# A top-k attention with a gated feed-forward: the feed-forward's steps in a fixed list over four slots

## The chip, the core and the metric

The kernel runs on one core of a Trainium2 chip, in one launch. Five engines run side by side, each through its own queue of instructions in the order in which the program issues them: TensorE (PE; PEld are its weight loads), VectorE (DVE), ScalarE (ACT), GpSimd (POOL) and SyncE (SP), which here issues DMAs. Where one engine needs what another makes, it waits on a semaphore. The metric is the device time of one execution in microseconds; lower is better. Three runs of the kernel before took 1398.21, 1399.92 and 1400.42 us, median 1399.92.

## What is computed

```python
batch, n_heads, seq, head_dim = (8, 8, 576, 64)
scores = scale * np.matmul(q, k.transpose(0, 1, 3, 2))
kth = np.partition(scores, -top_k, axis=-1)[..., -top_k:-top_k + 1]
scores = np.where(scores >= kth, scores, -1000000000.0)
attn = np.exp(scores - max); attn = attn / (sum + 1e-09)
x = (attn @ v), heads side by side        # 4608 tokens x 512
h = x @ w_in                              # 512 x 2048
g = h * np.cos(h)
out = g @ w_out                           # 2048 x 512
```

top_k is 32 of 576 keys. All is in fp32 (the weights are decoded on the chip from 64-bit words in the first slots).

## The kernel before

**Units, slots and blocks.** A unit is 128 tokens and one pair of heads (hp, 0 to 3): 144 units. Four units make a block of 128 tokens: 36 blocks. `slot(i, u, w, x, z)` (line 755) is called for i = 0 to 143, and its order of calls is the order in each engine's queue. Below, m = i mod 4. A slot carries several units at different stages: u = unit i is searched, w = unit i-1 is masked and exponentiated, x = unit i-2 is sent, z are the units whose values are due (from the second block on, a block's four units, in the slot with m = 2 three slots after that of its last unit).

**Attention, by engine.** `scores` (line 235, PE) writes two heads' scores of a unit into the PSUM tile `sc` (two buffers) and their last columns into `rim`, one PSUM tile of two banks whose rest holds the values of a block; from unit 4 on two units are scored together, in the slots with m = 0 and 2. `take_scores` (line 250, ACT) copies them into `s`: line 253 from `sc`, line 257, two instructions, from `rim`. VectorE folds the 576 scores of a row in two, `rest` (line 267, larger ones) and `low` (smaller ones, by two GpSimd passes, lines 283 and 292), and searches four rounds of eight in `rest` and two in `low` with MAX8 and MATCH_REPLACE8 (lines 359 and 364). One slot's search is most of VectorE's work, and the merge of line 347 opens the next. In slots 8 to 10 (`BUSY`) VectorE makes `low` itself. `mask` (line 374, ACT) sets apart what lies under the 32nd score and scales the small `nd`; `exponentials` (line 383, ACT) follow. `send` (line 740): GpSimd copies the result into `halves` (line 410) and the reciprocal of the sums beside it (line 412), SP writes that to DRAM (line 441), and a transposing DMA (line 447) brings it back into `ring`. From there PE forms the `values` (line 456) in `rim`, and `take_values` (VectorE, lines 491 and 499) multiplies them by the reciprocals into `xT`, in the `ahead` call between the two searches of `low`.

**The feed-forward.** Per block: four banks of the first product (`ff1`, line 554; two halves of a bank by two calls; PSUM tile `mm`), each taken by two ACT passes (`take_first`, lines 568 and 570: h in turns into `g`, the same rounded into `x` as an integer); for each pair of banks, 1024 columns, GpSimd converts the integer (line 590), subtracts it from g (line 599), ACT takes the sine (line 609; it needs another activation table than the exponentials, so a table load stands before it and before the next exponentials), GpSimd multiplies (`gate`, line 616). The second product (`ff2`, line 630; PSUM tile `o2`) sums sixteen pieces; two calls, 16 matmuls, are called a group here. `take_second` (lines 640 and 642, ACT) copies the result and issues its store on ACT's own DMA queue. `mm` and `o2` share two PSUM buffers, so that while `o2` is open one buffer is left for the banks.

**What sets the order.** Calls to `feed` at fixed places in the slot (`plan`, line 748) ask for steps of the first (0) or second (1) product; `can_first` and `can_second` (lines 647 and 655) grant them when the block is ready, weights are decoded and gates lie some ticks back; the second product is granted from slot 10 on (`ff["now"] < 2 * NP + 3`, with `now` = i + 1). Full banks wait in a queue for `take_banks`, which is called at several places; `reduce_first`, `reduce_second`, `sines` and `gate` take what is next. In the slots with odd i `sines(1)` stands ahead of `mask`. All of this is decided in Python while the program is built. After the last slot `drain` and `forward` (lines 825 and 815) work off the rest; there VectorE takes the place of GpSimd.

Of the kernel before, what the change touches and what calls it, by code (L numbers as in the profile page):

```python
# [30 lines left out]
def kernel(  # L31
# [64 lines left out]
    ff = {"live": 0, "tick": 0, "now": 0, "end": False, "kind": 0, "half": 0, "open": 0, "late": False}  # L96
# [213 lines left out]
    def topk_first(u, w):  # L310

        u["top"] = tops[u["n"] % len(tops)]
        if w:
            merge_first(w)
        if u["n"] not in BUSY:
            fold_sum(u)
        fold_high(u)
        if w:
            merge_second(w)
        if u["n"] in BUSY:  # L320
            fold_now(u)
        topk_round(u, 0, [lambda: distances(w), lambda: None] if w else ())
# [82 lines left out]
    def split(u):  # L405
# [3 lines left out]
        halves = work.tile([P, 2, 2 * S + P], U16, tag="halves", name="halves", bufs=1)  # L409
        nc.gpsimd.tensor_copy(out=halves[:, :, 0 : 2 * S], in_=s.rearrange("p (k h) -> p h k", h=2))  # L410
        rden = u.pop("rden").bitcast(U16).rearrange("p (j h) -> p h j", h=2)
# [4 lines left out]
        u["halves"] = halves  # L416
# [64 lines left out]
    def take_values(us):  # L481
# [23 lines left out]
        blk["left"] -= n  # L505
        blk["tick"] = ff["tick"]


    widths = [P] * (B * S // P)
    blocks, block_of = [], {}  # L510
    t0 = 0
    for w in widths:
        blk = {"t0": t0, "w": w, "left": 0, "g": [], "gated": []}
        for u in units:
            if t0 <= u["tok"] < t0 + w:
                block_of[u["tok"]] = blk
                blk["left"] += 1
        blocks.append(blk)
        t0 += w


    first = deque((blk, i) for blk in blocks for i in range(2 * NF * blk["w"] // 512))
    second = deque(
        (blk, i, f) for blk in blocks for i in range(blk["w"] // P) for f in range(0, NF, 2)
    )
    fresh = deque()
    waiting = deque()
    sined = deque()
    full = deque()

    def open_bank():

        if ff["open"] + len(full) == 2:
            take_banks()
        ff["open"] += 1

    def ff1(blk, i):
        w = blk["w"]
        nf = 256 // w
        part = i % 4  # L540
        if part == 0:
            blk["g"].append(ffw.tile([P, 1024], F32, tag="g", name="g", bufs=CHUNKS))
            blk["x"] = ffw.tile([P, 1024], F32, tag="x", name="x", bufs=XB)
            ff["live"] += 1
        if part % 2 == 0:
            open_bank()
            blk["mm"] = ps.tile([P, 512], F32, tag="mm", name="mm", bufs=2)
        g, mm = blk["g"][-1], blk["mm"]
        for a in range(nf):
            f = i * nf + a  # L550
            at = (part % 2 * nf + a) * w
            for c in range(NC):
                for r0 in range(0, P, D):
                    nc.tensor.matmul(  # L554
                        mm[r0 : r0 + D, at : at + w],
# [5 lines left out]
        if part % 2 == 0:  # L561
            return
        ff["open"] -= 1
        full.append((take_first, blk, g, blk["x"], mm, part // 2))

    def take_first(blk, g, x, mm, half):
        at = slice(half * 512, half * 512 + 512)
        nc.scalar.mul(out=g[:, at], in_=mm, mul=INV_2PI / UP)  # L568

        nc.scalar.activation(  # L570
            out=x[:, at].bitcast(I32), in_=mm, func=AF.Identity, bias=quarter, scale=INV_2PI / UP
        )
        if half == 1:
            fresh.append([blk, g, x, False, ff["now"] if ff["late"] else 0])

    def take_banks():
        while full:
            take, *what = full.popleft()
            take(*what)

    def reduce_first():

        if not fresh or (ff["late"] and not ff["end"] and fresh[0][4] == ff["now"]):
            return
        g, x = fresh[0][1:3]
        fresh[0][3] = True
# [5 lines left out]
        )  # L592

    def reduce_second():
        if not fresh or not fresh[0][3]:
            return
        blk, g, x, *_ = fresh.popleft()
        if not ff["end"]:
            nc.gpsimd.tensor_tensor(out=x, in0=g, in1=x, op=ALU.subtract)  # L599
        waiting.append((blk, g, x, ff["now"]))  # L600

    def sines(least):

        n = sum(c[3] < ff["now"] for c in waiting)
        if n == 0 or (n < least and waiting[0][3] + 2 > ff["now"]):
            return
        for _ in range(n):
            blk, g, x, _ = waiting.popleft()
            nc.scalar.activation(out=x, in_=x, func=AF.Sin, bias=halfpi, scale=TWO_PI_BELOW)
            sined.append((blk, g, x))  # L610

    def gate(n):
        for _ in range(min(n, len(sined))):
            blk, g, x = sined.popleft()
            eng = nc.vector if ff["end"] else nc.gpsimd
            eng.tensor_tensor(out=g, in0=g, in1=x, op=ALU.mult)  # L616
            blk["gated"].append(ff["tick"])

    def ff2(blk, i, f0):
        w = blk["w"]  # L620
        if f0 == 0:
            open_bank()
            blk["o"] = ps.tile([P, 512], F32, tag="mm", name="o2", bufs=2)
        o = blk["o"]
        per = 1024 // w
        for f in range(f0, f0 + 2):
            g = blk["g"][f // per]
# [275 lines left out]
```

## Time and profile before

| | |
|---|---|
| runs | 1398.21, 1399.92, 1400.42 us |
| profiled execution | 1399.15 us, span of its instructions 1397.0 us |
| granted TensorE clock | 0.974 of full on the mean, 1.00 from 120 us on |
| ACT, POOL busy | 1140.6 us (82%), 1169.3 us (84%) |
| DMA | 240.86 MB, mean 172 GB/s |

A row of the timeline gives the start in us from the span's first instruction, the duration, the engine, the line, the operation, the tiles written and read, their shapes, and how many instructions it merges; in brackets the idle time of the engine just before and what ended it. A row of a group gives busy time in us, the mean of one in ns, and idle time before them in total. A row of a stretch gives busy time and (in brackets) the number of instructions of PE, PEld, DVE, ACT and POOL, then the granted clock, the DMA engines' share and GB/s.

### The profile page before, as it was taken

Reading aid. Unit: us, or ns where it says so; the run is one execution under the profiler, and the core shown is the slowest. Engines: PE = TensorE matmul, PEld = TensorE weight load, DVE = VectorE, ACT = ScalarE, POOL = GpSimd, SP = SyncE. Lnnn points to the kernel's source line nnn. Section 1 sums busy time; section 2 is a strip of 40 time slices with the busy share of each in tenths; the row PEclk is TensorE's granted clock in tenths of the full one; section 3 lists DMA queues with packets and bytes.
Section 4 is the critical chain, followed back from the end, with each engine's and each line's share of the span. In section 5 each row is a group of like instructions: output and inputs, shape, how many; then the busy total and the mean of one; then the engine's idle time right before and its main releaser. Section 6 shows DMA issues by size and latency. Waiting matters only on the chain.

```text
span 1397.0 us, 43804 instructions
## 1 busy us (share of the span) xinstructions
PE 1339.6 (96%) x17024; PEld 905.7 (65%) x17024; DVE 1334.2 (96%) x5004; ACT 1140.6 (82%) x2043; POOL 1169.3 (84%) x804
## 2 busy tenths in 40 slices
PE   5558999999999999999999999999999999999998
PEld 3445666666666666666666666666666666666664
DVE  7999999999999999999999999999999999999931
ACT  7987888888888888888888888888888888888842
POOL 4778988889988888888988889888888898998820
PEclk6688999999999999999999999999999999999999
DMA  9566776777575586658756567676766566555530
GB/s 303 180 203 179 196 191 167 202 175 206 160 179 160 154 198 177 175 161 200 185 157 170 159 178 191 177 164 171 211 163 172 160 171 163 160 146 157 157 103 16
DMA packets 427487, 240.86 MB, mean 172 GB/s; under 512 B 375952, under 2 KB 392592, under 8 KB 427280
## 3 DMA queue, kind: packets, MB, share of 16 engines
q1 hardware_dynamic: 420720, 224.22, 61.0%
q10 hardware_dynamic: 6560, 13.85, 2.9%
q8 instruction: 133, 2.18, 0.7%
q14 instruction: 74, 0.61, 0.1%
HBM read 45.09 MB, written 101.19 MB: 105 GB/s over the span
## 4 chain that ended last, share of the span: by engine, by line
PE 59%; DVE 35%; ACT 2%; DMA 2%; POOL 1%; issue 1%; SPq 0%; DVEq 0%; POOLq 0%; ACTq 0%
PE o L630 23%; PE mm L554 23%; DVE top L359 16%; DVE rest L364 10%; PE rim L475 7%; PE sc L242 5%; DVE low L364 3%; DVE rest L267 3%; PE rim L242 1%; DMA ring<-rows 1%; DMA rows<-halves 1%; DVE xT L491 0%; DVE top L347 0%; DVE w_out L151 0%; DVE top L352 0%
## 5 line engine op out<-in xcount | busy, mean ns | idle before, releaser
L554 PEld LDWEIGHTS mm<-xT,w_in 128*64 128x64 f32 x9216 | 512.8, 137 | 85.1 <-issue 57.2
L554 PE MATMUL mm<-xT,w_in 128*64 128x128 f32 x9216 | 528.7, 273 | 3.2 <-DVE xT L491 2.1
L630 PE MATMUL o<-w_out,g 128*64 128x512 f32 x2304 | 520.0, 594 | 0.0
L359 DVE MAX8 top<-rest 128x8 f32<-128x288 f32 x1152 | 479.5, 452 | 0.0
L364 DVE MATCH_REPLACE8 rest<-top,rest 128x288 f32<-128x288 f32 x864 | 377.0, 444 | 0.0
L378 ACT ACTIVATE s<-s,top 128x576 f32<-128x576 f32 x288 | 207.7, 768 | 160.8 <-DVE top L352 157.8
L630 PEld LDWEIGHTS o<-w_out,g 128*64 128x64 f32 x2304 | 158.6, 137 | 254.1 <-issue 253.1
L410 POOL COPY halves<-s 128x2304 uint16<-128x2304 uint16 x140 | 294.8, 2106 | 29.1 <-ACT s L387 26.0
L359 DVE MAX8 top<-low 128x8 f32<-128x288 f32 x576 | 242.6, 452 | 0.4 <-POOL low L292 0.4
L387 ACT ACTIVATE s<-s,nd 128x576 f32<-128x576 f32 x288 | 220.5, 769 | 1.1
L292 POOL TENSOR_TENSOR low<-low,rest 128x576 int32<-128x576 int32 x141 | 199.6, 1416 | 11.1
L283 POOL TENSOR_TENSOR low<-s 128x576 int32<-128x576 int32 x141 | 199.7, 1417 | 6.1 <-ACT s L259 6.1
L599 POOL TENSOR_TENSOR x<-g,x 128x1024 f32<-128x1024 f32 x68 | 161.6, 2376 | 5.7
L242 PE MATMUL sc<-k,q 64*64 64x448 f32 (+1 forms) x1120 | 146.9, 568 | 16.9 <-DVE low L275 10.2
L616 POOL TENSOR_TENSOR g<-g,x 128x1024 f32<-128x1024 f32 x68 | 161.7, 2378 | 0.0
L475 PE MATMUL rim<-ring,v 128*64 128x128 f32 (+1 forms) x2560 | 138.3, 267 | 0.0
L475 PEld LDWEIGHTS rim<-ring,v 128*64 128x64 f32 x2560 | 129.2, 139 | 6.5 <-issue 6.0
L253 ACT COPY s<-sc 128x896 f32<-128x896 f32 (+1 forms) x144 | 128.4, 891 | 3.1 <-PE sc L242 3.1
L257 ACT COPY s<-rim 64x256 f32<-64x256 f32 (+1 forms) x280 | 102.9, 368 | 29.5 <-PE rim L475 27.9
L364 DVE MATCH_REPLACE8 low<-top,low 128x288 f32<-128x288 f32 x288 | 125.8, 446 | 0.0
L267 DVE TENSOR_TENSOR rest<-sc,s 128x576 f32<-128x576 f32 x144 | 107.7, 748 | 7.0 <-ACT s L259 6.4
L568 ACT ACTIVATE g<-mm 128x512 f32<-128x512 f32 x144 | 85.2, 592 | 25.7 <-PE mm L554 23.2
(55 smaller groups left out, 1161.8 us busy)
## 6 DMA issues: line engine op xcount, KB each, us to landing
rows<-halves SPq DMA_DIRECT2D x140, 640.0 KB, 3.5
out_dram<-ob ACTq DMA_DIRECT2D x36, 256.0 KB, 2.2
q<-in_q_dram SPq DMA_DIRECT2D x31, 288.0 KB, 4.6
st<-in_moe_w_in_dram SPq DMA_DIRECT2D x16, 512.0 KB, 5.1
v<-in_v_dram SPq DMA_DIRECT2D x32, 256.0 KB, 4.2
k<-in_k_dram SPq DMA_DIRECT2D x31, 144.0 KB, 4.2
k<-in_k_dram SPq DMA_DIRECT2D x32, 128.0 KB, 4.7
st<-in_moe_w_out_dram SPq DMA_DIRECT2D x8, 512.0 KB, 4.7
```

The lines of the kernel that those rows point to most:

```text
L242: nc.tensor.matmul(to[r0 : r0 + rows, rim_bank(r0, j) if k0 else place(u["hp"], j), 0 : k1 - k0], st["q"][d, q0 : q0 + rows], st["k"][d, k ...
L283: nc.gpsimd.tensor_tensor(out=u["low"].bitcast(I32), in0=s[:, :, 0:HS], in1=s[:, :, HS:S], op=ALU.add)
L292: nc.gpsimd.tensor_tensor(out=low, in0=low, in1=u["rest"][:, :, HS:S].bitcast(I32), op=ALU.subtract)
L359: nc.vector.max(to[:, j], src[:, j])
L364: nc.vector.match_replace(rest[:, j], to[:, j], src[:, j], NEG)
L378: nc.scalar.activation(out=s[:, j], in_=s[:, j], func=AF.Prelu, bias=less[:, j], scale=1.0, alpha=FAR)
L387: nc.scalar.activation(out=s[:, j], in_=s[:, j], func=AF.Exp, bias=nd[:, j : j + 1], scale=SCALE, accum_out=den[:, j, 0:1],)
L410: nc.gpsimd.tensor_copy(out=halves[:, :, 0 : 2 * S], in_=s.rearrange("p (k h) -> p h k", h=2))
L475: nc.tensor.matmul(to[d, r], lhsT, rhs, start=(bank, j) not in begun, stop=c == NT - 1 and u in us[-2:] and r0 + rows == P,)
L554: nc.tensor.matmul(mm[r0 : r0 + D, at : at + w], w_in[f // FC][:, c, (f % FC) * P + r0 : (f % FC) * P + r0 + D], blk["xT"][:, c], start=c ...
L616: eng.tensor_tensor(out=g, in0=g, in1=x, op=ALU.mult)
L630: nc.tensor.matmul(o[r0 : r0 + D], g[:, at + r0 : at + r0 + D], w_out[f], start=f == 0, stop=f == NF - 1)
```

## The change

The planner (queues, `plan`, `feed`, `can_first`, `can_second`, `forward`) goes. `slot` now names each step of the feed-forward with its block and its place. Block b, with b = (i - 6) // 4, has its first bank at the end of a slot with m = 2, the second at the end of m = 3, the third in m = 0 behind the scores and the previous block's last group, the fourth in m = 1 right after it in TensorE's order, followed by its own first group. Arguments and gates work on one bank (512 columns) at a time, sines on two. The second product's first group stands in slot 9 for block 0. In the slot with m = 2 the second sine and two gates stand between `exponentials` and `take_scores`; in m = 0 the first sine and `take_second` close the slot. `split` falls into two functions that are called one after the other. Weight loads after slot 5 go by the list 2, 2, 0, 2, 2, 0 in slots 6 to 11 where up to 2 a slot were tried from slot 6 on, with slot 9 left out. `drain` is written out.

```diff
-    def topk_first(u, w):
+    def topk_first(u, w, ahead=()):
...
 
         u["top"] = tops[u["n"] % len(tops)]
         if w:
             merge_first(w)
+        for step in ahead:
+            step()
         if u["n"] not in BUSY:
             fold_sum(u)
         fold_high(u)
...
+    def half_of(tiles, k):
+        return tiles[k // 2][:, k % 2 * 512 : k % 2 * 512 + 512]
...
+    def first_bank(b, k):
...
+        if k == 0:
+            blk["g"], blk["x"], blk["mm"] = [], [], {}
+        if k % 2 == 0:
             blk["g"].append(ffw.tile([P, 1024], F32, tag="g", name="g", bufs=CHUNKS))
+            blk["x"].append(ffw.tile([P, 1024], F32, tag="x", name="x", bufs=XB))
             ff["live"] += 1
+        mm = blk["mm"][k] = ps.tile([P, 512], F32, tag="mm", name="mm", bufs=2)
+        for a in range(PER):
+            f = k * PER + a
+            assert wq["done"] >= (f // FC + 1) * NC
             for c in range(NC):
                 for r0 in range(0, P, D):
                     nc.tensor.matmul(
+                        mm[r0 : r0 + D, a * P : (a + 1) * P],
                         w_in[f // FC][:, c, (f % FC) * P + r0 : (f % FC) * P + r0 + D],
                         blk["xT"][:, c],
                         start=c == 0,
                         stop=c == NC - 1,
                     )
+    def take_first(b, k):
...
+        mm = blk["mm"].pop(k)
+        nc.scalar.mul(out=half_of(blk["g"], k), in_=mm, mul=INV_2PI / UP)
         nc.scalar.activation(
+            out=half_of(blk["x"], k).bitcast(I32), in_=mm, func=AF.Identity, bias=quarter, scale=INV_2PI / UP
+        )
+    def argument(b, k):
...
+        g, x = half_of(blk["g"], k), half_of(blk["x"], k)
         if ff["end"]:
             nc.vector.tensor_tensor(out=x, in0=g, in1=x.bitcast(I32), op=ALU.subtract)
             return
         nc.gpsimd.tensor_scalar(
             out=x, in0=x.bitcast(I32), scalar1=1.0, scalar2=0.0, op0=ALU.mult, op1=ALU.add
         )
+        nc.gpsimd.tensor_tensor(out=x, in0=g, in1=x, op=ALU.subtract)
+    def sine(b, t):
...
+        x = blk["x"][t]
+        nc.scalar.activation(out=x, in_=x, func=AF.Sin, bias=halfpi, scale=TWO_PI_BELOW)
+    def gate(b, k):
...
+        g, x = half_of(blk["g"], k), half_of(blk["x"], k)
+        eng = nc.vector if ff["end"] else nc.gpsimd
+        eng.tensor_tensor(out=g, in0=g, in1=x, op=ALU.mult)
+    def second_run(b, r):
...
+        if r == 0:
             blk["o"] = ps.tile([P, 512], F32, tag="mm", name="o2", bufs=2)
+        for f in range(r * PER, (r + 1) * PER):
+            g = half_of(blk["g"], f // PER)
+            assert wq["done"] > NC * NF // FC + f
             for r0 in range(0, P, D):
+                at = f % PER * P + r0
                 nc.tensor.matmul(
+                    blk["o"][r0 : r0 + D], g[:, at : at + D], w_out[f], start=f == 0, stop=f == NF - 1
                 )
+    def take_second(b):
...
         ob = ffw.tile([P, DM], F32, tag="ob", name="ob", bufs=1)
+        nc.scalar.mul(out=ob, in_=blk.pop("o"), mul=2.0 * math.pi / UP)
+        row = blk["t0"]
         nc.scalar.dma_start(out=out[row : row + P, :], in_=ob)
+        ff["live"] -= len(blk.pop("g"))
+        blk.pop("x")
...
     def slot(i, u, w, x, z):
-        n = (3, 4, 3, 4, 4, 3)[i] if i < NP + 2 else 2 if i != 2 * NP + 1 else 0
+        m, b = i % NP, (i - NP - 2) // NP
+        n = (3, 4, 3, 4, 4, 3, 2, 2, 0, 2, 2, 0)[i] if i < 3 * NP else 0
         if i < NP:
-            for load, b, hp in at_once[i]:
-                load(b, hp)
+            for load, bb, hp in at_once[i]:
+                load(bb, hp)
         load_weights(n, nc.sync if i < NP + 2 else nc.scalar)
         if x:
             (turn if i < NP + 2 else send)(x)
-        ff["late"] = False
-        topk_first(u, w)
+        if m == 1:
+            gate(b, 0)
+        elif m == 0:
+            argument(b, 0)
+        topk_first(u, w, [lambda: argument(b - 1, 3)] if m == 2 else ())
         fold_low(u)
         topk_round(u, 1)
         topk_round(u, 2)
         if i > 1:
             decode_second(NP)
             decode_third()
-        reduce_first()
-        reduce_second()
-        made = scored.get(i, [])
-        if z:
-            take_banks()
-        feed(*((0, 0) if i == NP + 2 else plan[i % NP][0]))
-        for m in made:
-            scores(m)
+        for o in scored.get(i, []):
+            scores(o)
         if z:
             values(z)
-        if i % 2:
-            sines(1)
+        if m == 1:
+            gate(b, 1)
+        elif m == 0:
+            second_run(b - 1, 3)
+        elif m == 2:
+            second_run(b - 1, 1)
+        elif m == 3:
+            second_run(b - 1, 2)
         if w:
             mask(w)
-        if i % NP != 3:
-            take_banks()
+        if m == 0:
+            take_first(b, 1)
+            argument(b, 1)
+            first_bank(b, 2)
+        elif m == 1:
+            take_first(b, 2)
+            argument(b, 2)
+            first_bank(b, 3)
+            second_run(b, 0)
         if w:
             exponentials(w)
-        take_banks()
+        if m == 3:
+            take_first(b, 0)
+        elif m == 2:
+            sine(b - 1, 1)
+            gate(b - 1, 2)
+            gate(b - 1, 3)
         if i + 1 < NU:
             take_scores(units[i + 1])
         def ahead():
             if z:
                 take_values(z)
         if i == 0:
             decode_second(NP)
             decode_third()
-        ff["late"] = True
-        gate(1)
-        feed(*plan[i % NP][1])
-        take_banks()
+        if m == 2:
+            first_bank(b, 0)
+        elif m == 3:
+            first_bank(b, 1)
+        elif m == 0:
+            sine(b, 0)
+            take_second(b - 1)
+        elif m == 1:
+            take_first(b, 3)
         decode_first(NP)
-        reduce_first()
-        reduce_second()
-        feed(*plan[i % NP][2])
...
+    def drain():
+        b = NB - 2
+        ff["end"] = True
+        w, x, last_two = units[NU - 1], units[NU - 2], units[NU - 2 :]
+        send(x)
+        argument(b, 0)
+        second_run(b - 1, 3)
+        merge_first(w)
+        merge_second(w)
+        distances(w)
+        mask(w)
+        exponentials(w)
+        sums(w)
+        reciprocal(w)
+        send(w)
+        take_first(b, 1)
+        argument(b, 1)
+        first_bank(b, 2)
+        sine(b, 0)
+        gate(b, 0)
+        gate(b, 1)
+        take_second(b - 1)
+        take_first(b, 2)
+        first_bank(b, 3)
+        argument(b, 2)
+        second_run(b, 0)
+        take_first(b, 3)
+        argument(b, 3)
+        second_run(b, 1)
+        sine(b, 1)
+        gate(b, 2)
+        gate(b, 3)
+        values(units[NU - 4 : NU - 2])
+        take_values(units[NU - 4 : NU - 2])
+        second_run(b, 2)
+        values(last_two)
+        take_values(last_two)
+        second_run(b, 3)
+        b += 1
+        first_bank(b, 0)
+        take_second(b - 1)
+        take_first(b, 0)
+        argument(b, 0)
+        for k in range(1, BANKS):
+            first_bank(b, k)
+            take_first(b, k)
+            argument(b, k)
+            if k % 2 == 1:
+                sine(b, k // 2)
+                gate(b, k - 1)
+                gate(b, k)
+        for r in range(BANKS):
+            second_run(b, r)
+        take_second(b)
```

219 lines of the change are left out of this document (36 added, 183 removed).

## The prediction

> **What bounds the kernel now.** I read the page first, then busy time by stretches, the timeline of one cycle engine by engine, and the end.
>
> ```profile
> span 1397.0 us, 43804 instructions
> PE 1339.6 (96%) x17024; PEld 905.7 (65%) x17024; DVE 1334.2 (96%) x5004; ACT 1140.6 (82%) x2043; POOL 1169.3 (84%) x804
> 200.00:300.00 100.00, 100.00 (x1362) 67.69 (x1360) 100.00 (x380) 84.90 (x156) 88.78 (x62) 1.00 0.67 178
> 1200.00:1300.00 100.00, 100.00 (x1384) 68.66 (x1382) 100.00 (x382) 84.00 (x153) 88.34 (x61) 1.00 0.55 154
> ```
>
> From 200 to 1300 us VectorE and TensorE are both busy throughout at full clock. A cycle of four slots, m = 0 to 3 (slot number modulo 4), takes one block through. The merge of line 347 marks the start of a slot on VectorE.
>
> ```profile
> 767.90 0.23 DVE L347 TENSOR_REDUCE top<-top 128x34 f32<-128x68 f32 x1
> 774.35 0.81 DVE L359 MAX8 top<-low 128x8 f32<-128x288 f32 x2
> 775.91 0.69 DVE L491 TENSOR_TENSOR xT<-rim,ring 128x512 f32<-128x512 f32 x1
> 777.42 0.23 DVE L347 TENSOR_REDUCE top<-top 128x34 f32<-128x68 f32 x1
> 786.35 0.23 DVE L347 TENSOR_REDUCE top<-top 128x34 f32<-128x68 f32 x1
> 767.83 0.98 PE L242 MATMUL sc<-k,q 64*64 64x448 f32 x8
> 769.86 0.62 PE L475 MATMUL rim<-ring,v_tail 64*64 64x128 f32 x16
> 773.96 3.60 PE L630 MATMUL o<-w_out,g 128*64 128x512 f32 x16
> 777.39 3.66 PE L554 MATMUL mm<-xT,w_in 128*64 128x128 f32 x64
> 780.88 3.60 PE L630 MATMUL o<-w_out,g 128*64 128x512 f32 x16
> ```
>
> Slot 82 (m=2) lasts 777.42 - 767.90 = 9.52 us, as it holds xT; the next lasts 8.93. A cycle of VectorE is 9.52 + 3 x 8.93 = 36.3 us. TensorE needs, from start to start, 2.03 for two units' scores (twice), 4.10 for the values, 3.43 for a group of the second product (o), 3.49 for a bank of the first (mm): 4.06 + 4.10 + 4 x 3.43 + 4 x 3.49 = 35.8 us. So VectorE sets the pace with 0.5 us to spare on TensorE, and whatever makes VectorE wait costs its full length, 32 times over (slots 18 to 142). The end is TensorE's alone:
>
> ```profile
> 1331.85 0.23 DVE L347 TENSOR_REDUCE top<-top 128x34 f32<-128x68 f32 x1
> 1329.67 3.71 PE L554 MATMUL mm<-xT,w_in 128*64 128x128 f32 x64
> 1379.33 13.90 PE L630 MATMUL o<-w_out,g 128*64 128x512 f32 x64
> ```
>
> (The last row is the final 64 matmuls in one piece.) VectorE is through with slot 143 at 1331.85, TensorE stops at 1393.23: 61.4 us later.
>
> **Part 1: one group less at the end.** The old plan opens the second product in slot 10, the new list at the end of slot 9. Both then do four groups a cycle, so at slot 143's end the old order still owes ten groups and six banks, the new one nine and six: -3.43. In the new drain the third bank must wait for its predecessor to be emptied: by the steps of Part 2 the mask comes 1.05 after VectorE's end, exponentials at 2.6, take_first from 4.2 to 5.3; the group ahead of that bank ends at 1.5 (1329.67 + 3.71 less 1331.85) + 3.43 = 4.9: +0.4. Later banks alternate with 3.4 us of TensorE between them, and sine plus two gates (under 3 us) hide beneath two banks. Sum **-3.0**; bounds -3.9 and -2.
>
> **Part 2: ScalarE in the slot m=2.** Today the score copies come ahead of the sine; the new list puts sine(b-1,1) between the exponentials and the copies, and the bank's take moves out to m=1. VectorE's xT reads the PSUM tile rim, which the copy of line 257 reads too, and it waits for that copy:
>
> ```profile
> 118.90 0.49 DVE L499 TENSOR_TENSOR xT<-rim,ring 128x128 f32<-128x128 f32 x2 [1.19 <-ACT s L257]
> 156.75 0.74 ACT L257 COPY s<-rim 64x256 f32<-64x256 f32 x2 [1.89 <-PE rim L475]
> 157.53 0.76 DVE L491 TENSOR_TENSOR xT<-rim,ring 128x256 f32<-128x256 f32 x2 [0.67 <-ACT s L257]
> 130.87 0.76 DVE L267 TENSOR_TENSOR rest<-sc,s 128x576 f32<-128x576 f32 x1 [0.57 <-ACT s L257]
> ```
>
> The copy ended at 157.49, xT began 0.04 later. So the new place of the copy is a price, and I add it up from the slot's start.
>
> ```profile
> 768.98 1.44 ACT L378 ACTIVATE s<-s,top 128x576 f32<-128x576 f32 x2 [1.26 <-DVE top L352]
> 770.33 0.19 ACT L381 ACTIVATE nd<-nd 128x2 f32<-128x2 f32 x1
> 771.47 0.77 ACT L387 ACTIVATE s<-s,nd 128x576 f32<-128x576 f32 x1
> 772.89 0.20 ACT L387 ACTIVATION_READ_ACCUMULATOR s<-s,nd 128x1 f32 x1
> 772.98 0.89 ACT L253 COPY s<-sc 128x896 f32<-128x896 f32 x1
> 774.17 0.74 ACT L257 COPY s<-rim 64x256 f32<-64x256 f32 x2 [0.30 <-PE rim L475]
> 774.93 1.28 ACT L609 ACT_TABLE_LOAD   x1
> 776.23 1.15 ACT L609 ACTIVATE x<-x,halfpi 128x1024 f32<-128x1024 f32 x1
> 779.79 0.19 ACT L381 ACTIVATE nd<-nd 128x2 f32<-128x2 f32 x1
> 780.00 1.28 ACT L387 ACT_TABLE_LOAD   x1
> ```
>
> Mask at 1.08, nd at 2.43. What needs nd follows 0.21 later (779.79 to 780.00): exponentials at 2.64. Their last accumulator read ends 772.89 + 0.20 - 771.47 = 1.62 after their start: 4.26. Load 0.02 later (as behind line 257), sine 1.30 after that: 5.58, ending at 6.73. Instructions of ScalarE follow up to 0.09 before the former one ends (770.33 against 768.98 + 1.44): copy of line 253 at 6.64, line 257 at 6.64 + 0.80 = 7.44, done at 8.18. With 0.04, xT starts at 8.22 where it starts at 775.91 - 767.90 = 8.01 now: VectorE **waits 0.2 us a cycle**, 32 x 0.2 = **+6.4**. Behind xT stand the low search's second half and all later slots. Bounds: 0.08 if mask and exponentials each start some 0.06 earlier, 0.31 if the copy follows the sine's end without overlap (each +2.6 and +9.9). I take 0.2, where each step has its own row.
>
> A load that stands behind an accumulator read is not in these rows, and that opens a rival. The Trainium skill (ScalarE: Activation LUTs, What ACT_TABLE_LOAD costs) has a switch at 1283 ns for the load and about 1380 ns more to drain, 2.66 us in all. The trace agrees with the load and shows no drain: 0.02 us ahead of it, 0.02 behind. By the page the wait would be 1.58 us a cycle and the sum about 47 us more than mine.
>
> **Part 3: GpSimd, in half passes.** VectorE, ScalarE and TensorE keep their instructions in number and size; what the planner did in Python leaves none behind. On GpSimd arguments and gates now run per bank: 512 columns, four of each a cycle where there were two of each at 1024. From the reciprocal that opens m=0 to the low search of m=2 GpSimd has no pause left, so this stretch is summed.
>
> ```profile
> 777.51 0.40 POOL L412 COPY halves<-rden 128x256 uint16<-128x256 uint16 x1 [0.30 <-DVE rden L400]
> 777.88 1.42 POOL L283 TENSOR_TENSOR low<-s 128x576 int32<-128x576 int32 x1
> 779.37 1.42 POOL L292 TENSOR_TENSOR low<-low,rest 128x576 int32<-128x576 int32 x1
> 780.74 2.39 POOL L616 TENSOR_TENSOR g<-g,x 128x1024 f32<-128x1024 f32 x1
> L410 POOL COPY halves<-s 128x2304 uint16<-128x2304 uint16 x140 | 294.8, 2106 | 29.1 <-ACT s L387 26.0 <-DMA rows<-halves 3.1
> L590 POOL TENSOR_SCALAR x<-x 128x1024 f32<-128x1024 int32 x68 | 71.1, 1046 | 30.0 <-ACT x L570 30.0
> L599 POOL TENSOR_TENSOR x<-g,x 128x1024 f32<-128x1024 f32 x68 | 161.6, 2376 | 5.7
> L160 POOL TENSOR_TENSOR w_out<-w_out,st 128x512 int32<-128x512 int32 x16 | 20.3, 1297 | 16.4 <-ACT s L387 5.2 <-issue 4.2 <-ACT st L136 3.5
> ```
>
> It starts 0.09 into m=0 (777.51). Old pieces: three small copies of 0.37, two splits of 2.05 (2.106 less the 0.05 by which independent passes overlap, 779.37 + 1.42 against 780.74), three first folds of 1.49, two second folds of 1.37 and the last, 1.42: 14.0 with the start. A half two-input pass is a row of its own, the 512-wide 1.297 of line 160, spaced 1.25. The half conversion (1.046 at 1024) lies between 0.52 and, with a fixed part of 0.2 as the two copies give, 0.62, and its reader follows 0.07 after its end: 0.69. Four arguments of 1.94 and two gates of 1.25 are 10.26; in all 24.2 us. The low search needs it 2 x 8.93 + 6.45 = 24.3 after the start of m=0 (774.35 - 767.90 = 6.45). It fits with **0.1 us to spare: no cost**. The bounds: clean halves leave 1.1; passes as long as the 576-wide neighbours (1.37) come 0.6 late. A lateness below 0.2 also vanishes under Part 2's wait, which stands later in the same slot.
>
> **Part 4: what lies under cover.** The store of a finished block and its take go to the end of m=0; with its issue on ScalarE's queue they push the mask of m=1 from 1.02 to 1.3 and that slot's copies to 8.4, needed at 9.0 by the next slot's fold. Without that 0.6, each 0.1 beyond it would cost 3.2 us. In m=3 the halves are written some 1.5 us later on SP's queue, with loads and transposes behind them; the rows are read a cycle later, and m=1's, read first, are written no later than now. Groups behind the scores and two banks in a row are the same work on TensorE; its 0.5 us hide the 0.2 by which the second bank waits for its predecessor's take. Early on, by the new pace of loads, the decode of slot 9 moves to slot 10 and under the 1.19 us wait of row 118.90:
>
> ```profile
> L151 DVE TENSOR_SCALAR w_out<-w_out 128x1024 int32<-128x1024 int32 x7 | 5.8, 844 | 0.0
> ```
>
> Less what overlaps, I take -0.6 for it. GpSimd comes into slots 12 and 14 late as it does now, by the same pieces 0.3 less in sum: together **-0.9**, bounds -2.4 (1.19 + 0.57 + 0.67, all early waits gone) and +1.5 (GpSimd's lateness in both slots 0.75 longer).
>
> Sum: 6.4 - 3.0 - 0.9 = +2.5 us on 1397.0. The profiled execution took 1399.15 with what lies around its span, 0.8 under the median of the three runs, 1399.92; I put the 2.5 on the median: **1402.4 us**.
>
> **Rivals.** *No wait at xT, then faster.* If the copies end by 7.97, only -3.0 and -0.9 remain: 1396.0. For it: 0.2 is small beside steps read to 0.1. Against: two early blocks show the wait and each step has a row.
> *GpSimd misses the low search, then slower.* The mechanism is Part 3's chain; its place the low search in m=2; it decides from the point where four arguments and two gates exceed 10.6 (lateness over 0.2). Half-way to its bound, 0.4 late: 32 x 0.4 - 3.9 = +8.9, 1408.8; at the bound 1415. For it: a margin of 0.1. Against: the 512-wide row.
> *TensorE becomes the bound.* The fourth bank needs the buffer that o leaves; its take stands behind the sine and ends 0.9 us into m=1, TensorE arrives at 1.4. If arguments make that sine over 1 us late, TensorE has more to wait than its spare 0.5 + 0.2; at 1.2 us of wait the cycle is 37.0, 0.7 x 32 - 3.9 = +18.5, 1418. Against: the argument is done at 7.2, the table loaded at 8.1.
> *The load drains the exponentials.* A drain as long as the load, 1.28, ahead of the sine makes Part 2's wait 1.48: 47.4 - 3.9 = +43.5, 1443. Against: the gaps of 0.02.
>
> **How the numbers follow.** About 0.2% (2.8 us) is what a measurement of this kernel can tell from no change. Forecast 0.58, with its own range 1397 to 1407.5 from the bounds of Part 2: 0.02 faster, 0.37 same, 0.19 slower. No wait 0.14, nearly all faster. GpSimd late 0.16, TensorE 0.09, drain 0.03, all slower. Together faster 0.15, same 0.38, slower 0.47. The range takes in the no-wait case and GpSimd's half price: 1395.5 to 1410.
>
> **What would show it.** Right: xT idle about 0.2 us before it on the copy of line 257 in each m=2 slot, that slot 9.7 long and the others 8.93; the second fold's end some 6.3 into m=2 with no wait at the low search; TensorE's last matmul about 58 us after VectorE's slot 143. Wrong: m=2 slots of 9.52 (the no-wait case), waits of VectorE on low, idle of TensorE in m=1 on the take of o, or a gap around the sine's table load.

## The result, and the profile after

Twelve runs of the changed kernel took 1404.76 to 1407.78 us, median **1406.12**; twelve of the kernel before 1398.21 to 1405.79, median 1399.95. The ratio after to before is **1.0040** (95% interval 1.0029 to 1.0051): slower by 0.3 to 0.5%, some 6 us. Forecast were 1402.4 us, in a range of 1395.5 to 1410. The profiled execution took 1406.25 us, 7.1 us more than that of before.

The page of the changed kernel, span and busy times, then the shares of its chain of waits:

```profile
span 1404.1 us, 43874 instructions
...
PE 1347.3 (96%) x17024; PEld 906.3 (65%) x17024; DVE 1337.5 (95%) x5012; ACT 1140.7 (81%) x2043; POOL 1197.8 (85%) x1008
...
DVE 68%; ACT 18%; PE 8%; POOL 3%; issue 1%; DMA 1%; ACTq 0%; POOLq 0%; DVEq 0%
```

The shares of the kernel before:

```profile
PE 59%; DVE 35%; ACT 2%; DMA 2%; POOL 1%; issue 1%; SPq 0%; DVEq 0%; POOLq 0%; ACTq 0%
```

VectorE and ScalarE now carry 86% of the chain, 37% before. VectorE's busy time grew by 3.3 us only; the rest is waiting. The timeline of slot 82 (m=2), VectorE and GpSimd, and then ScalarE, shows where it waits:

```profile
774.44 0.23 DVE L349 TENSOR_REDUCE top<-top 128x34 f32<-128x68 f32 x1
779.32 1.42 POOL L292 TENSOR_TENSOR low<-low,rest 128x576 int32<-128x576 int32 x1
780.89 0.80 DVE L361 MAX8 top<-low 128x8 f32<-128x288 f32 x2
782.64 0.69 DVE L496 TENSOR_TENSOR xT<-rim,ring 128x512 f32<-128x512 f32 x1
784.16 0.23 DVE L349 TENSOR_REDUCE top<-top 128x34 f32<-128x68 f32 x1
...
775.52 1.45 ACT L380 ACTIVATE s<-s,top 128x576 f32<-128x576 f32 x2 [0.52 <-DVE top L354]
777.08 0.78 ACT L389 ACTIVATE s<-s,nd 128x576 f32<-128x576 f32 x1
778.53 0.19 ACT L389 ACTIVATION_READ_ACCUMULATOR s<-s,nd 128x1 f32 x1
778.73 1.28 ACT L583 ACT_TABLE_LOAD   x1
780.03 1.15 ACT L583 ACTIVATE x<-x,halfpi 128x1024 f32<-128x1024 f32 x1
781.09 0.88 ACT L253 COPY s<-sc 128x896 f32<-128x896 f32 x1
781.87 0.74 ACT L257 COPY s<-rim 64x256 f32<-64x256 f32 x2
```

From the slot's start at 774.44 the mask comes at +1.08, the exponentials at +2.64, the table load at +4.29, the sine at +5.59, the two copies at +6.65 and +7.43, xT at +8.20. The prediction had 1.08, 2.64, 4.28, 5.58, 6.64, 7.44 and 8.22. The slot lasts 784.16 - 774.44 = 9.72 us instead of 9.52. The second fold ends at 780.74, +6.30, and the low search behind it does not wait. The end, on VectorE and TensorE:

```profile
1341.73 0.67 DVE L570 TENSOR_TENSOR x<-g,x 128x512 f32<-128x512 f32 x1
1342.31 0.21 DVE L349 TENSOR_REDUCE top<-top 128x34 f32<-128x68 f32 x1
...
1386.44 13.90 PE L606 MATMUL o<-w_out,g 128*64 128x512 f32 x64
```

TensorE stops at 1400.34, 58.0 us after VectorE's merge (61.4 before). Some 0.54 of that is given back: the drain's first argument (line 570) now stands ahead of the merge.

Slot by slot (from one merge to the next), the two profiles differ in few places:

| | before | after | difference, us |
|---|---|---|---|
| up to slot 1 | 16.85 | 17.25 | +0.40 |
| slot 9 | 10.16 | 9.55 | -0.61 |
| **slot 10** | **11.56** | **15.41** | **+3.85** |
| slot 12 | 9.66 | 9.29 | -0.37 |
| slot 14 | 10.46 | 10.56 | +0.10 |
| 32 slots m=2, from 18 on | 9.59 mean | 9.79 mean (9.78 without slot 130) | +6.4 (0.18 of it is slot 130's own) |
| slot 143 and after it | | | +0.54 - 3.35 |

Together +7.0, and 0.1 in hundredths over the other slots. (Slots 5 and 6 trade 0.76 between them. The start of slot 1 lies between 16.1 and 17.3 us in all profiles of this document, so its 0.40 is no price of the change.) All but slot 10 is as forecast or small. In slot 10, the timeline of the kernel after:

```profile
96.23 2.56 POOL L160 TENSOR_TENSOR w_out<-w_out,st 128x512 int32<-128x512 int32 x2 [3.27 <-ACT s L257]
99.45 1.28 POOL L575 TENSOR_TENSOR x<-g,x 128x512 f32<-128x512 f32 x1
100.68 2.10 POOL L412 COPY halves<-s 128x2304 uint16<-128x2304 uint16 x1
100.77 1.15 ACT L583 ACTIVATE x<-x,halfpi 128x1024 f32<-128x1024 f32 x1 [3.65 <-POOL x L575]
100.77 0.82 ACTq L120 DMA_DIRECT2D st<-in_moe_w_out_dram  x2
103.15 0.34 SPq L446 DMA_DIRECT2D rows<-halves  x1
107.20 2.92 SPq L452 DMA_TRANSPOSE ring<-rows  x1
108.77 0.23 DVE L349 TENSOR_REDUCE top<-top 128x34 f32<-128x68 f32 x1
108.95 0.33 ACTq L120 DMA_DIRECT2D st<-in_moe_w_out_dram  x1
116.00 0.58 PE L480 MATMUL rim<-ring,v_tail 64*64 64x128 f32 x4 [3.48 <-DMA ring<-rows]
116.51 5.19 PE L480 MATMUL rim<-ring,v 128*64 128x128 f32 x64
121.75 0.74 ACT L257 COPY s<-rim 64x256 f32<-64x256 f32 x2 [2.98 <-PE rim L480]
122.53 0.49 DVE L504 TENSOR_TENSOR xT<-rim,ring 128x128 f32<-128x128 f32 x2 [4.38 <-ACT s L257]
```

and the same stretch of the kernel before:

```profile
98.34 2.11 POOL L410 COPY halves<-s 128x2304 uint16<-128x2304 uint16 x1
100.81 0.34 SPq L441 DMA_DIRECT2D rows<-halves  x1
103.97 3.90 SPq L447 DMA_TRANSPOSE ring<-rows  x1
113.80 4.28 PE L475 MATMUL rim<-ring,v 128*64 128x128 f32 x64
118.12 0.74 ACT L257 COPY s<-rim 64x256 f32<-64x256 f32 x2 [3.99 <-PE rim L475]
```

Read backwards: xT waits for the copy of line 257, the copy for the values in the same tile, the values for unit 7's transposed transfer (ring<-rows). Counted from slot 10's start (108.77, before 108.98), the values begin 2.9 us later (+7.74 against +4.82) and the copy comes after them 0.9 later still. Unit 7's rows go out 2.55 later (-5.62 against -8.17), because GpSimd's split stands behind argument(0,1), and that behind the weights' third pass (line 160). The rows then took 4.0 us to land instead of 3.0, the transposed transfer 8.8 instead of 9.2 (the view of DMA issues over that moment). What among these decides was open: lateness on GpSimd, the DMA engines shared with the weights, or TensorE's clock.

### The profile page after: what moved, and what is told of

Its sections match the earlier page's. It is cut to its first block, busy times and chain, and to the rows that moved or that the text cites. A ratio compares the mean times of both kernels' runs of the same rounds, so it can differ in the third digit from the quotient of the medians.

```text
span 1404.1 us, 43874 instructions
## 1 busy us (share of the span) xinstructions
PE 1347.3 (96%) x17024; PEld 906.3 (65%) x17024; DVE 1337.5 (95%) x5012; ACT 1140.7 (81%) x2043; POOL 1197.8 (85%) x1008
## 4 chain that ended last, share of the span: by engine, by line
DVE 68%; ACT 18%; PE 8%; POOL 3%; issue 1%; DMA 1%; ACTq 0%; POOLq 0%; DVEq 0%
DVE top L361 32%; DVE rest L366 18%; DVE rest L267 7%; DVE low L366 6%; ACT s L389 4%; ACT s L380 4%; PE o L606 3%; ACT L583 3%; PE mm L543 3%; ACT x L583 2%; ACT s L253 2%; PE rim L480 2%; ACT s L257 2%; DVE xT L496 1%; DMA ring<-rows 1%
## 5 line engine op out<-in xcount | busy, mean ns | idle before, releaser
L592 POOL TENSOR_TENSOR g<-g,x 128x512 f32<-128x512 f32 x136 | 172.5, 1279 | 16.4 <-ACT x L583 16.4
L575 POOL TENSOR_TENSOR x<-g,x 128x512 f32<-128x512 f32 x136 | 174.0, 1279 | 11.4
L242 PEld LDWEIGHTS rim<-k,q 64*64 64x64 f32 (+1 forms) x1120 | 49.0, 139 | 75.6 <-issue 60.1
```

Source lines behind the costliest of these rows:

```text
L242: nc.tensor.matmul(to[r0 : r0 + rows, rim_bank(r0, j) if k0 else place(u["hp"], j), 0 : k1 - k0], st["q"][d, q0 : q0 + rows], st["k"][d, k ...
```

## The experiments

In each, VectorE's slots tell where a time went. Ratios are against runs of the kernel before on the same chip (medians 1400.1 and 1399.79 us).

**The copies first.**

```diff
         if m == 1:
             gate(b, 0)
         elif m == 0:
             argument(b, 0)
+        elif m == 3:
+            gate(b - 1, 2)
         topk_first(...)
         fold_low(u)
+        if m == 3:
+            gate(b - 1, 3)
...
-        elif m == 2:
-            sine(b - 1, 1)
-            gate(b - 1, 2)
-            gate(b - 1, 3)
         if i + 1 < NU:
             take_scores(units[i + 1])
+        if m == 2:
+            sine(b - 1, 1)
```

> Score copies ahead of the sine again in slots m=2; gates of chunks 2 and 3 in slot m=3. Theory (VectorE's xT waits 0.2 us for ScalarE's last score copy, 32 times): slots m=2 take 9.52 us again instead of 9.72, no idle time at xT, 32 x 0.2 = 6.4 us less than the changed kernel: 1399 to 1400 us. Rival A (the 0.2 us is GpSimd's lateness in another place): the low search waits in the slots m=2 instead, time 1405 to 1407. Rival B (TensorE needs the gated chunks earlier than m=3 gives them): idle time of TensorE before the matmuls of the third or fourth run in m=3 or m=0, time above 1407.

Measured: 1400.9 us (1396.87 to 1403.12, 12 runs), ratio to before 0.9999 [0.9991, 1.0008]. The groups of xT from 200 to 1300 us (behind the last bar: idle time before them), in the kernel after:

```profile
L496 DVE TENSOR_TENSOR xT<-rim,ring 128x256 f32<-128x256 f32 (+1 forms) x36 | 17.9, 510 | 2.5
L504 DVE TENSOR_TENSOR xT<-rim,ring 128x128 f32<-128x128 f32 x24 | 5.8, 283 | 0.8 <-ACT s L257 0.3
```

and with the copies first:

```profile
L496 DVE TENSOR_TENSOR xT<-rim,ring 128x256 f32<-128x256 f32 (+1 forms) x36 | 17.6, 504 | 0.0
L504 DVE TENSOR_TENSOR xT<-rim,ring 128x128 f32<-128x128 f32 x24 | 5.8, 283 | 0.0
```

The wait is gone and the slots m=2 are back at 9.52 to 9.68 (mean 9.59): 6.4 us, as Part 2 had them. Neither rival shows: the low search waits for nothing, and the banks' matmuls were held up 0.0 us from 200 to 1300 us. The median fell by 5.2, and the runs spread over 6 us where the changed kernel's spread over 3. The profiled execution was the fastest of the twelve, with a slot 10 of 12.19.

**Slot 8's order on GpSimd.**

```diff
         if i > 1:
             decode_second(NP)
-            decode_third()
+            if i != 2 * NP:
+                decode_third()
...
         if m == 0:
             take_first(b, 1)
             argument(b, 1)
+            if i == 2 * NP:
+                decode_third()
```

> In slot 8 alone the weights' third pass stands behind argument(0,1) on GpSimd instead of ahead of it. Theory (slot 10's 3.85 us come from the split of unit 7 that starts late behind argument(0,1), which itself stood behind the third pass): that split starts about 98.7 instead of 100.7, the rows' transfers are issued about 2 us sooner, slot 10 is 2 to 4 us shorter: 1402 to 1404 us. Rival (the transfers of slot 10 are late because weights and rows share the DMA engines, whenever the rows are issued): slot 10 stays at 15.4 us, 1406 us.

Measured: 1406.81 us, ratio 1.0047 [1.0035, 1.0059]; slot 10 took 15.72. Slot 10 is no shorter, but the edit does not test GpSimd's order alone. The rows did go out at 101.04 instead of 103.15, but argument(0,1) also frees sine(0,0) on ScalarE, and behind that sine stand the weights' transfers of slot 9, on ScalarE's own queue: issued at 94.86 instead of 100.77. The DMA issues of that moment (the last number is us from issue to landing):

```profile
st<-in_moe_w_out_dram ACTq DMA_DIRECT2D x2, 512.0 KB, 7.3
ring<-rows SPq DMA_TRANSPOSE x1, 13.8
```

They fell on unit 6's transposed transfer, which took 13.8 us (4.9 in the kernel after), and unit 7's rows, issued behind it on the same queue, took 8.8. One lateness was exchanged for another.

**Both edits**, with argument(b - 1, 3) moved from its place in `topk_first` to behind `fold_low`.

> The two edits of e1 and e2 together, and argument 3 moved behind the second fold in m=2. Theory: the gains add, 6.4 + 2 to 4 us: 1396 to 1398 us, below the kernel before by 2 to 4 us. Rival (slot 10's lateness and the waits share cover, so that one gain eats the other): 1399 us or more.

Measured: 1399.95 us, ratio 1.0000 [0.9989, 1.0011]. The slots m=2 are short, and slot 10 took 19.87 us in the profiled execution (1403.89 us, one of the slowest of its twelve): the theory's sum failed by slot 10, as in the run before.

**The second product a run later.**

```diff
         elif m == 0:
-            second_run(b - 1, 3)
+            second_run(b - 1, 2)
         elif m == 2:
-            second_run(b - 1, 1)
+            second_run(b - 1, 0)
         elif m == 3:
-            second_run(b - 1, 2)
+            second_run(b - 1, 1)
...
             argument(b, 2)
+            second_run(b - 1, 3)
             first_bank(b, 3)
-            second_run(b, 0)
...
             sine(b, 0)
-            take_second(b - 1)
         elif m == 1:
+            take_second(b - 1)
             take_first(b, 3)
...
 def drain():
         argument(b, 0)
-        second_run(b - 1, 3)
+        second_run(b - 1, 2)
...
         first_bank(b, 2)
+        second_run(b - 1, 3)
         sine(b, 0)
```

> All four runs of the second product one slot later, so that one group more is left for the end. Theory (the groups left at the end count with their whole TensorE time of 3.4 us there, and nothing in the slots): TensorE ends about 61.4 us after VectorE's last round instead of 58.0, slots as in the changed kernel, 1409 to 1410 us. Rival (the end is set by ScalarE and VectorE, and the group disappears in their waits): 58 us, 1406 us.

Measured: 1417.86 us, ratio 1.0129 [1.0114, 1.0144]: more than expected. The expectation's own part holds in direction: TensorE stops 62.4 us after VectorE's last merge, 58.0 in the kernel after, so the run costs 4.3 at the end, 0.9 more than its TensorE time of 3.43. The rest was overlooked: `take_second` now stands ahead of `take_first(b, 3)` at the end of m=1, ScalarE's mask in m=2 comes at +1.31 instead of +1.08, and every step behind it as much later. The slots m=2 grew by 0.23 (mean 10.02), and xT's groups, 200 to 1300 us, read:

```profile
L496 DVE TENSOR_TENSOR xT<-rim,ring 128x256 f32<-128x256 f32 (+1 forms) x36 | 17.9, 511 | 8.0 <-ACT s L257 8.0
L504 DVE TENSOR_TENSOR xT<-rim,ring 128x128 f32<-128x128 f32 x24 | 5.8, 284 | 2.0 <-ACT s L257 2.0
```

0.23 us later on ScalarE is 0.23 later on VectorE, each cycle: Part 2's chain once more, from its other end. 4.3 and 32 x 0.23 make 11.7, the measured difference from the changed kernel.

**The weights' transfers earlier.** Two runs, each with one line changed:

```diff
-        n = (3, 4, 3, 4, 4, 3, 2, 2, 0, 2, 2, 0)[i] if i < 3 * NP else 0
+        n = (3, 4, 3, 4, 4, 3, 2, 2, 2, 2, 0, 0)[i] if i < 3 * NP else 0    # first run
+        n = (3, 4, 3, 4, 4, 3, 2, 2, 2, 0, 2, 0)[i] if i < 3 * NP else 0    # second run
```

> The changed kernel with the last two of the weights' transfers issued in slot 8 in place of slot 10 (transfers per slot 2, 2, 2, 2, 0, 0 from slot 6 on in place of 2, 2, 0, 2, 2, 0), nothing else. Theory (slot 10 is long because unit 7's transposed transfer shares the DMA engines with the two weights' transfers issued behind it: 8.76 us in place of 4.9): that transfer takes about 5 us and lands near 112 instead of 116, the wait at slot 10's xT falls from 4.38 to under 0.5 us, slot 10 takes 11 to 11.5 us: 1402 to 1403 us. Rival (unit 7's transfer is long because unit 8's rows go out beside it): slot 10 stays above 14 us, 1405 us or more.

> The changed kernel with the transfers of slot 9 moved to slot 8 (2, 2, 2, 0, 2, 0), those of slot 10 left where they are. Theory (the transfers of slot 10 are the ones that collide): unit 7's transposed transfer still takes 8 to 9 us, slot 10 still 14 to 15.4 us: 1405 to 1406 us. Rival (the transfers of slot 9, which hold back unit 7's rows by 0.9 us and the two passes on GpSimd, are what moved): slot 10 takes 11.5 us as in the kernel before: 1402 us.

Measured: 1403.73 us (1403.24 to 1404.86), ratio 1.0031 [1.0018, 1.0043]; and 1404.05 us, ratio 1.0032 [1.0020, 1.0044]. In the first run no weights' transfer stands beside unit 7's transposed one. Its DMA issue:

```profile
ring<-rows SPq DMA_TRANSPOSE x1, 5.0
```

So 5.0 us without them and 8.1 in the second run, with the two transfers of slot 10 beside it. Unit 8's rows, the rival of the first expectation, stand beside neither (they went out at 114.38, and at 113.93 behind a landing at 113.68), so they are not needed for a long transfer. But slot 10 does not follow in either case as expected: 13.10 us in the first run, 11.03 in the second, which is the rival's number there. In both, slot 9 grew by 1.5 us (11.09 and 11.08): VectorE's decode stands in it again (0.6), and ScalarE now decodes two chunks ahead of that slot's mask, so that VectorE waits 0.8 us for its exponentials there and 0.65 for its copies at the start of slot 10. Slot 10 begins that much later beside the same transfer.

The second run's list is the pace of the kernel before, whose transfers also stand in slots 6, 7, 8 and 10. With it slots 9 and 10 together take 22.1 us, 21.7 in the kernel before and 25.0 in the kernel after, and the median falls by 2.1. So most of the lengthening goes with the new pace of loads.

And in the first run ScalarE sets slot 10's wait, though unit 7's transfer had landed at 112.49 and the values, 3.71 us long, began at 114.29. Its timeline:

```profile
117.72 1.28 ACT L583 ACT_TABLE_LOAD   x1
119.01 1.15 ACT L583 ACTIVATE x<-x,halfpi 128x1024 f32<-128x1024 f32 x1
120.06 0.89 ACT L253 COPY s<-sc 128x896 f32<-128x896 f32 x1
120.85 0.74 ACT L257 COPY s<-rim 64x256 f32<-64x256 f32 x2
121.63 0.49 DVE L504 TENSOR_TENSOR xT<-rim,ring 128x128 f32<-128x128 f32 x2 [1.37 <-ACT s L257]
```

That is the sine ahead of the copies again, in slot 10.

**Copies first and transfers early**: the first edit and (2, 2, 2, 2, 0, 0) together.

> Score copies ahead of the sine in slots m=2 (as in e1_copies_first) and the transfers of e4_loads_early. Theory (the two causes are apart and add): no wait at xT in the slots m=2, 6.4 us, and a short slot 10, about 3 to 4 us: 1395 to 1397 us, 3 to 5 us below the kernel before, with a narrower spread from run to run than e1_copies_first. Rival (the copies' order alone already takes the wait of slot 10 away): 1400 to 1401 us, as e1_copies_first.

Measured: **1395.44 us** (1395.28 to 1396.05, 6 runs), ratio 0.9968 [0.9956, 0.9979]: 4.4 us below the kernel before, 10.7 below the change, and all its runs within 0.8 us. Slots 9 to 14 sum to 59.1 us, 63.3 in the kernel after. Without both waits the list is 0.2 to 0.4% faster than the planner. The two gains do not simply add: by the medians the copies alone brought 5.2 us, the transfers alone 2.4, both together 10.7. The causes meet in slot 10, where the transfers alone leave VectorE waiting for the copies behind the sine (13.10), and the copies alone leave it waiting for unit 7's transfer.

**GpSimd's small copy twice.**

```diff
-        nc.gpsimd.tensor_copy(
-            out=halves[:, :, 2 * S :].rearrange("p h (j d) -> p h j d", j=2),
-            in_=rden.unsqueeze(3).to_broadcast([P, 2, 2, D]),
-        )
+        n = u["n"] + 2
+        for _ in range(2 if n > 4 * NP and n % NP == 1 else 1):
+            nc.gpsimd.tensor_copy(...)
```

> The changed kernel with GpSimd's small copy of the reciprocals issued twice in the slots m=1 from slot 17 on: 0.37 us more in GpSimd's chain ahead of slot m=2's low search, 32 times. Theory (0.14 us to spare there, and a lateness takes the place of the 0.2 us wait at xT behind it): the low search waits 0.2 to 0.25 us, the wait at xT is gone, slots m=2 grow by 0.03 to 0.05 us: 1407 to 1408 us. Rival (the two waits add, since ScalarE's copies are late with the low search): slots m=2 grow by 0.2 us or more: 1412 us or more.

Measured: 1411.43 us, ratio 1.0091 [1.0071, 1.0112]; slots m=2 of 9.96 on the mean, 0.18 more. Their groups from 200 to 1300 us:

```profile
L361 DVE MAX8 top<-low 128x8 f32<-128x288 f32 x480 | 202.1, 450 | 8.2 <-POOL low L292 8.2
...
L498 DVE TENSOR_TENSOR xT<-rim,ring 128x256 f32<-128x256 f32 (+1 forms) x36 | 17.6, 504 | 0.0
```

One wait takes the place of the other: the low search waits and xT no longer does. A sum of both would have been 0.2 + 0.37, not 0.37 in all over 9.59. That is the theory's mechanism, but the size and the time are nearly the rival's (0.2 us, 1412): the second copy, equal to the first, took 0.46, not 0.37 (both together 0.86), and the fold ended at +6.76 in its slot instead of +6.30.

**Three kernels again, unedited**, for slot 10.

> The changed kernel once more, unedited, for slot 10 alone. Theory (slot 10 is long in every execution, since its runs lie within 3 us of each other): unit 7's transposed transfer takes 7 us or more, slot 10 takes 14 to 16 us. Rival (slot 10's 15.41 us were one execution's accident, and the median hides another cost): slot 10 takes 12 us or less at the same total.

> The kernel before once more, unedited, for slot 10 alone. Theory: slot 10 is about 11.6 us and slots 9 and 10 together about 21.7 us, as in the first profile. Rival (the first profile caught a short slot 10): together 23 us or more.

> The kernel of e1_copies_first once more, unedited, for slot 10 alone: its twelve times lie between 1396.9 and 1403.1 us, and the profiled one was the lowest. Theory (unit 7's transposed transfer and the granted clock of the values behind it differ from run to run): a slot 10 of 13 to 16 us with a transfer of 8 us or more or values of 5 us, at a total near 1400. Rival (the spread lies elsewhere): slot 10 is 12 us again.

Measured: 1406.58, 1400.65 and 1402.57 us. The changed kernel came out by the theory. The kernel before lies between its two expectations (22.4 us), and the copies first went beyond theirs (17.97 us in slot 10). With the earlier profiles:

| kernel | unit 7's transposed transfer, us | values' 64 matmuls, us | slot 10, us | slots 9 and 10, us |
|---|---|---|---|---|
| before | 9.2 and 7.3 | 4.28 and 4.97 | 11.56 and 12.22 | 21.7 and 22.4 |
| after | 8.8 and 9.1 | 5.19 and 5.36 | 15.41 and 15.73 | 25.0 and 25.3 |
| copies first | 7.2 and 10.0 | 3.71 and 5.20 | 12.19 and 17.97 | 21.8 and 27.5 |
| slot 8's order | 6.2 | 5.10 | 15.72 | 25.3 |
| both edits | 12.4 | 5.13 | 19.87 | 29.4 |
| a run later | 8.5 | 3.71 | 13.54 | 23.1 |
| small copy twice | 6.9 | 3.71 | 12.28 | 21.8 |
| transfers early | 5.0 | 3.71 | 13.10 | 24.2 |
| slot 9 empty (the old pace) | 8.1 | 3.71 | 11.03 | 22.1 |
| copies first, transfers early | 5.1 | 3.71 | 11.64 | 22.7 |

Slot 10 is long in both executions of the changed kernel. But it need not be: the kernel with the small copy twice has the same instructions as the changed one up to slot 16, and there slot 10 took 12.28, with a wait at xT of 1.24 us in place of 4.38. Against the first profile of the kernel after, its transposed transfer landed 1.9 us earlier in the slot, TensorE had idled 1.97 us in place of 3.48, and the values took 1.5 less. An unedited run with such a slot would come to about 1403 us; none of its thirteen times lies below 1404.76. The kernel with the copies first swings by 5.8 in that one slot, about the spread of its times (6.3). No one column sets the slot: behind a transfer of 8.1 us slot 10 is the shortest, as slot 9 had taken the time before. The second length, that of the values, goes with TensorE's idle time ahead of them: in the faster of the two executions of the copies first

```profile
114.30 0.44 PE L480 MATMUL rim<-ring,v_tail 64*64 64x128 f32 x4 [2.27 <-DMA ring<-rows]
114.67 3.71 PE L480 MATMUL rim<-ring,v 128*64 128x128 f32 x64
```

and in the slower one

```profile
117.83 0.69 PE L480 MATMUL rim<-ring,v_tail 64*64 64x128 f32 x4 [5.94 <-DMA ring<-rows]
118.45 5.20 PE L480 MATMUL rim<-ring,v 128*64 128x128 f32 x64
```

The stretch from 116 to 119 us in the kernel after (the number behind POOL's is the granted clock):

```profile
116.00:119.00 3.00, 3.00 (x28) 2.68 (x30) 2.15 (x8) 2.75 (x3) 3.00 (x3) 0.53 0.11 43
```

and in the faster execution of the copies first:

```profile
116.00:119.00 3.00, 3.00 (x48) 2.50 (x46) 2.03 (x8) 0.70 (x3) 3.00 (x3) 1.00 0.12 42
```

After 2.27 us of idle the clock stays at 1.00; after 3.48 (and 4.14, 5.94) it is near half, and the same 64 matmuls take 1.5 to 1.7 us more.

## Why the prediction came out as it did

| part | forecast, us | in the profiles, us |
|---|---|---|
| 1, one group less at the end | -3.0 | -2.8 (-3.35 + 0.54) |
| 2, xT behind the late copies | +6.4 | +6.2 |
| 3, GpSimd in half passes | 0 | 0 |
| 4, what lies under cover, early slots | -0.9 | +3.0 |
| nowhere forecast | | +0.6 (0.40 up to slot 1, 0.18 in slot 130) |
| sum | +2.5 | +7.0 (7.1 with the hundredths of the other slots) |

The likeliest case came true. The median lies 3.7 us above the forecast; between the two profiles it is 4.6, of which Part 4 makes 3.9. That the time still lies in the range is luck as far as Part 4 goes: its sign was wrong, and the width of the range came from other parts and cases.

**Part 2** held to 0.02 us at each step, and it was shown by taking it away (copies first: 32 slots back to 9.59) and by making it longer (a run later: +0.23 for 0.23). The drain that the Trainium skill (ScalarE: Activation LUTs, What ACT_TABLE_LOAD costs) adds to a table load is not there: 778.53 + 0.19 ends the accumulator read, 778.73 begins the load, 1.28 us, and 0.02 later the sine stands. That rival is out. (By the prediction's own terms the page's figure would add 32 x 1.38 = 44 us, not "about 47".) The one without a wait would have come to 1396.0; with the wait removed and slot 10 repaired the kernel does reach 1395.44.

**Part 3** held: the chain ends at +6.30 in slot 82, as forecast ("some 6.3"), and 0.15 ahead of the search. The doubled copy shows how thin that is: with 0.46 us more on GpSimd the search waits, in place of xT. The prediction's clause that a small lateness would vanish under Part 2's wait agrees with it, since 0.46 cost 0.18.

**Part 1** held in direction and nearly in size. The third bank's wait in the drain, put at 0.4, was 0.34 (TensorE, 1347.15); the 0.54 in slot 143 was not foreseen. The run moved back cost 4.3 at the end.

**Part 4** is the step that was mis-sized: "by the new pace of loads, the decode of slot 9 moves to slot 10 and under the 1.19 us wait of row 118.90". The decode did move (slot 9: -0.61), and slots 12 and 14 gained 0.27 together, as written. But the 1.19 us wait was taken as cover (time in which VectorE waits anyway) of fixed length, with its cause not followed upstream. Its cause is unit 7's transposed transfer; the new list puts an argument ahead of that unit's split on GpSimd and sends weights in slot 9 as well as in slot 10, and the wait grew to 4.38 us. The upper bound of +1.5 counted GpSimd's lateness in slots 12 and 14 alone, so it was no bound for slot 10. By the rows the transfer lands 3.0 us later in the slot than in the kernel before: the rows go out 2.55 later and take 1.0 more to land, with slot 9's weights issued beside them, while the transposed transfer is 0.4 shorter. So its sharing with slot 10's weights, which the kernel before has too, is a price but not the difference. TensorE's clock adds to it: the values take 5.19 us behind the longer idle, 4.28 before, 3.71 at full clock. With the old pace of loads slots 9 and 10 are back at 22.1. What an earlier split alone would save stays open, since the decode moved behind it brought the transfers forward as well, and so does why the same instructions gave 12.28 once and over 15 twice. That copies and transfers repaired together bring slots 9 to 14 down is shown.

**TensorE as the bound** did not come: from 200 to 1300 us the banks' matmuls of the kernel after were held up 0.8 us in all.

## What to carry to other kernels

Follow a wait that is to serve as cover back to what ends it, and ask whether the change touches that chain too; cover is not of fixed length. On an engine where others read the same tile behind it, the order of two independent steps is a price per cycle, and it can be added up to hundredths from rows of neighbouring slots. Where one queue carries both work and the issue of transfers, releasing the work early releases the transfers early, and they may land on something worse.

## What the runs showed of the hardware

- The idle time that a record shows is less than what the wait costs. The groups of xT in the kernel after hold 2.5 + 0.8 = 3.3 us for 30 cycles, 0.11 each, while the slots grew by 0.20; with a run later 10.0, 0.33 each, for 0.43; the low search with the copy twice 8.2, 0.27 each, for 0.37. The difference of 0.09 to 0.10 is about the overlap by which an instruction of VectorE that waits for nothing starts ahead of the former one's end (in slot 82 one of 0.75 us began at 774.58, the next at 775.24).
- From 130 us on, where no weights are transferred, the transposed transfers take 4.4 to 8.1 us, with medians of 4.9 to 5.1 in the profiles here. Those issued between 80 and 110 us with two weights' transfers between 0.9 us before and 2.5 us behind their issue took 6.9 to 12.4, and one 13.8.
- TensorE's granted clock stayed at 1.00 over 2.27 us of idle and stood near half (0.53) after 3.48. The Trainium skill (TensorE: Matmul & The Clock Gate, Part 1: The HAM clock gate) has the clock halved after an idle window of about 3.4 us; the rows agree, and they give the price here: the same values 3.71 or 5.19 us. In the kernel after the clock was still 1.00 over that idle time, fell to 0.50 from 116.16 to 119.58, when TensorE was already at work again, and was 1.00 behind that.
